# Scoring the last 64 keys in two row halves, and moving twelve PSUM copies from ScalarE to VectorE

## The chip, the cores and the metric

The kernel runs on 1 core of one Trainium2 chip. The metric is the time of one execution on the device, in microseconds (us), of which lower is better. The program ran three times; the profile is of a further execution of its own. Everything below is about one core with five engines: TensorE (PE, with its weight loads as PEld), VectorE (DVE), ScalarE (ACT), GpSimd (POOL) and SyncE (SP). All data is float32 at the interface; most products are made from "high" and "low" parts of type float32r (three products for one), the weights times v product in plain float32.

## What is computed

Sigmoid attention over 4 batches, 12 heads, 448 positions and head size 64, then two dense blocks on the 1792 x 768 result:

```
scores = q @ k.T / sqrt(64) - log(448)          # per batch and head
attn   = 1 / (1 + exp(-scores));  x = attn @ v  # x is 1792 x 768 after joining the heads
h = max(x @ w1, x @ w2, x @ w3);  y = h @ w_out             # first block, d_ff 768
h = y @ w_in;  sm = exp(h - max(h)) / (sum + 1e-9)          # second block, d_ff 1024
ln = normalise(h * sm) * g_ln;    out = ln @ w_out2
```

## The kernel before

The heads are taken in pairs: 24 pairs (6 per batch), each a **visit**, numbered 0 to 23 here. In SBUF a pair's q and k lie with head 0 in partitions 0 to 63 and head 1 in partitions 64 to 127 (64 dimensions each). The 448 keys are cut into blocks of 128: c = 0, 1, 2 are whole, and c = 3 holds the last 64 keys. The k array has 512 columns for this: columns 384 to 447 hold head 0's last keys with zeros in the lower half of the rows, columns 448 to 511 hold head 1's with zeros in the upper half.

For one visit the order on PE is: the four score blocks in the order 3, 0, 1, 2 (the function `scores`, lines 246 to 266), then the products with v (`attend`, line 278): blocks 1 and 2 of the pair before, then blocks 3 and 0 of this pair. A score block is three products (high-high, low-high, high-low). For c = 0, 1, 2 each is two matmuls (line 257), one per head on its own 64 rows of the array, into two PSUM banks; the two run side by side. For c = 3 each is one matmul over all 128 rows (line 253), since the zeros keep the heads apart, into one bank. The PSUM pool `ps_sc` has 3 buffers of two banks, so a visit's fourth score block needs the buffer of its first; `ps_av` has 2 buffers of one bank.

ACT turns each score block into weights `sf` with a sigmoid: 128 x 896 for c = 0, 1, 2 (line 265), 128 x 448 for c = 3 (line 262, with a buffer of its own). After a pair's last product with v, `take_x` (from line 286) takes the 128 x 448 result `av` out of PSUM: ACT writes its high part (B11h, B21h or B22h), DVE the low part (B11l, ...), and for the even batches (0 and 2) ACT also copies it to T1f or T4f in float32. For the odd batches DVE makes differences with those copies.

Between the two halves of the attention (visits 0 to 11 and 12 to 23) PE makes the product of two weight matrices, `pw` (line 469). Its operands `wi_t` and `r_wo` are prepared during visits 2 to 11: per piece one ACT instruction (line 155) and four on DVE (lines 159, 163, 54, 57), two pieces in a visit. Visit 12's scores stand inside the last part of `pw`. In the second half, background steps (splits of the T arrays, conversion of the last weights with pieces `w2s` that go out to DRAM through two staging buffers, conversion of the next group) are spread between the visits' steps.

PE, ACT and DVE run their instructions in the order in which the program is written. After the attention, from 201.20 us, come the Strassen-like products of the first block and the second block.

Of the kernel before, what the change touches and what calls it, by code (L numbers as in the profile page):

```python
# [7 lines left out]
F32 = mybir.dt.float32  # L8
F32R = mybir.dt.float32r
I32 = mybir.dt.int32  # L10
AF = mybir.ActivationFunctionType
# [5 lines left out]
P = 128  # L17
B, H, S, D = 4, 12, 448, 64
# [27 lines left out]
def sigmoid_attention_max_moe_solu_ln(tc, q, k, v, w123, wo, wi, w2, g, out):  # L46
    nc = tc.nc
    pe, act, dve, pool, sp = nc.tensor, nc.scalar, nc.vector, nc.gpsimd, nc.sync

    def copy(eng, dst, src):  # L50
        if eng is act:
            act.copy(dst, src)
        else:
            eng.tensor_copy(dst, src)

    def rest(eng, dst, src, hi):
        eng.tensor_tensor(out=dst, in0=src, in1=hi.bitcast(F32), op=ALU.subtract)  # L57

    def tt(dst, a, b, op):
        dve.tensor_tensor(out=dst, in0=a, in1=b, op=op)  # L60

    def open_pool(name, bufs, side="left", space=None):
        kw = dict(name=name, bufs=bufs, side=side)
        if space is not None:
            kw["space"] = space
        cm = tc.tile_pool(**kw)
        return cm, cm.__enter__()
# [22 lines left out]
    a_cm, apool = open_pool("apool", 2)  # L90
# [3 lines left out]
    bias_s = const.tile([P, 1], F32, name="bias_s")  # L94
# [111 lines left out]
    def f_tile(nm, i, name):  # L206
        return fpool.tile([P, S], F32, tag=f"{nm}_{i}", name=name)
# [16 lines left out]
    def load_v(pr):  # L224
        if pr >= NP:
            return
        vr = apool.tile([P, 2, 4, D], F32, tag="vr", name=f"vr{pr}", bufs=3)
        sp.dma_start(out=vr, in_=v[pr])
        v_ops[pr] = vr
# [16 lines left out]
    def scores(pr, c):  # L246
        qt, kt = qk_ops[pr]
        sc = ps_sc.tile([P, 2, 512], F32, tag="sc", name=f"sc{pr}_{c}")
        terms = ((0, 0), (1, 0), (0, 1))
        for t, (x, y) in enumerate(terms):  # L250
            start, stop = t == 0, t == len(terms) - 1
            if c == 3:
                pe.matmul(sc[:, 0, :S], lhsT=kt[:, x, c * P :], rhs=qt[:, y], start=start, stop=stop)
                continue
            for j in range(2):
                rows = slice(j * D, (j + 1) * D)
                pe.matmul(  # L257
                    sc[:, j, :S], lhsT=kt[rows, x, c * P : (c + 1) * P], rhs=qt[rows, y], start=start, stop=stop
                )
        if c == 3:  # L260
            sf = apool.tile([P, S], F32, tag="s3", name=f"sf{pr}_{c}", bufs=1)
            act.activation(sf, sc[:, 0, :S], AF.Sigmoid, bias=bias_s, scale=1.0 / math.sqrt(D))  # L262
        else:
            sf = apool.tile([P, 2, S], F32, tag="sf", name=f"sf{pr}_{c}", bufs=5)
            act.activation(sf, sc[:, :, :S], AF.Sigmoid, bias=bias_s, scale=1.0 / math.sqrt(D))  # L265
        weights[(pr, c)] = sf

    pas = {}
# [1 line left out]
    def attend(pr, n):  # L270
        vr = v_ops[pr]
        c = BLOCKS[n]
        if n == 0:
            pas[pr] = ps_av.tile([P, 512], F32, tag="av", name=f"av{pr}")
        pa = pas[pr]
        sf = weights.pop((pr, c))
        for j in range(2):
            pe.matmul(  # L278
                pa[j * D : (j + 1) * D, :S],
                lhsT=vr[:, j, c],  # L280
                rhs=sf if c == 3 else sf[:, j],
                start=(n == 0),
                stop=(n == 3),
            )
        if n == 3:
            v_ops.pop(pr)
            load_v(pr + 3)

    def take_x(pr):
        pa = pas.pop(pr)[:, :S]  # L290
        b, hp = divmod(pr, NPAIR)
        bp, odd = divmod(b, 2)
        half, i = divmod(hp, 3)
        f = {nm: fts.get((bp, nm, i)) for nm in TS}

        def new(nm):
            t = fts[(bp, nm, i)] = f_tile(nm, i, f"{nm}f{bp}_{i}")
            return t

        nm = (("B11", "B21"), (None, "B22"))[odd][half]  # L300
        if nm:
            hi, lo = xops[bp][(nm, i)]
            copy(act, hi, pa)
            rest(dve, lo, pa, hi)
        if not odd:
            copy(act, new("T4" if half else "T1"), pa)
        elif not half:
            copy(act, new("T3"), pa)
            tt(f["T1"], pa, f["T1"], ALU.subtract)
        else:  # L310
            t2 = new("T2")
            tt(t2, pa, f["T1"], ALU.subtract)
            tt(f["T3"], pa, f["T3"], ALU.subtract)
            tt(f["T4"], f["T4"], t2, ALU.subtract)
# [27 lines left out]
    def visit(pr, n_conv):  # L342
        for n, c in enumerate(BLOCKS):
            scores(pr, c)
            if n == 1:
                prep_qk(pr + 1)
        finish_conv()
        attend_rest(pr, n_conv)
# [12 lines left out]
    def attend_rest(pr, n_conv, steps=0):  # L361
        if pr > 0 and pr - 1 in pas:
            attend(pr - 1, 2)
            run_bg(steps)
            attend(pr - 1, 3)
            run_bg(steps)
            take_x(pr - 1)
        attend(pr, 0)
        run_bg(steps)
        attend(pr, 1)  # L370
        run_bg(steps)
        begin_conv(n_conv)
# [23 lines left out]
    attend(MID - 1, 3)  # L396
    finish_conv()
    take_x(MID - 1)
    assert not conv

# [84 lines left out]
    for fc in range(FC):  # L485
        for n in range(2):
            if (fc, n) == (FC - 1, 1):
                for i, c in enumerate(BLOCKS):
                    scores(MID, c)
                    if i == 1:  # L490
                        prep_qk(MID + 1)
            while not {("wo", fc, 0), ("wo", fc, 1)} <= ready:
                run_bg()
            gen_w(fc, n)
        slots.pop(("wo", fc, 0))
        slots.pop(("wo", fc, 1))
# [67 lines left out]
    for pr in range(MID + 1, NP):  # L564
        for n, c in enumerate(BLOCKS):
            scores(pr, c)
            if n == 1:
                prep_qk(pr + 1)
            run_bg()
        attend_rest(pr, 0, 1)  # L570
        run_bg(2)
    attend(NP - 1, 2)
    attend(NP - 1, 3)
    take_x(NP - 1)
    run_bg(1 << 20)
    for cm, _ in reversed(ps1):
# [449 lines left out]
```

## Time and profile before

| | before |
|---|---|
| median of 3 runs | 664.98 us (662.64 to 666.3) |
| the profiled execution | 661.11 us |
| span of its profile | 659.3 us |
| busy: PE, DVE, ACT | 650.7 us (99%), 484.0 us (73%), 318.4 us (48%) |

The span counts from the first recorded instruction to the last; the 1.8 us between 659.3 and 661.11 lie around it. Busy PE time says only that some matmul was in flight. The granted clock of TensorE was 1.00 in every slice.

### The profile page before, as it was taken

The numbers are of one execution on the slowest core, as the hardware profiler recorded it, in microseconds if no ns is written. First come the engines' busy times: TensorE is split into PE (matmuls) and PEld (weight loads), VectorE is DVE, ScalarE is ACT, GpSimd is POOL, SyncE is SP. The second block draws the span as 40 slices with busy tenths as digits, with TensorE's granted clock in tenths as the row PEclk, the third lists the DMA queues.
The fourth block names the chain that finished last, engine by engine and source line by source line (L and its number), as shares of the span: only waits on it lengthen the run. The fifth ranks groups of instructions, "written<-read, shape, count | busy, mean of one in ns | idle before, by whom it ended". The sixth has DMA issues, their size and how long they took to land.

```text
span 659.3 us, 9629 instructions
## 1 busy us (share of the span) xinstructions
PE 650.7 (99%) x3370; PEld 534.1 (81%) x3370; DVE 484.0 (73%) x1051; ACT 318.4 (48%) x642; POOL 58.0 (9%) x112
## 2 busy tenths in 40 slices
PE   9999999999999999999999999999999999999997
PEld 5555588754458999999999999978989898989897
DVE  4799988688758786775787577638959595868583
ACT  5888534587876534534444444315424242433242
POOL 1111121001110101100101100022000000000000
PEclk9999999999999999999999999999999999999999
DMA  8688769956540215534335422899743323323231
GB/s 295 215 261 255 214 208 330 325 179 197 162 128 1 96 67 175 167 113 134 106 108 205 120 70 91 286 357 408 273 143 99 115 93 116 99 77 115 61 113 48
DMA packets 53328, 109.16 MB, mean 166 GB/s; under 512 B 5952, under 2 KB 34656, under 8 KB 52512
## 3 DMA queue, kind: packets, MB, share of 16 engines
q1 hardware_dynamic: 44208, 64.48, 29.3%
q0 software_dynamic: 8928, 43.85, 20.3%
q8 instruction: 26, 0.43, 0.3%
q10 hardware_dynamic: 144, 0.23, 0.1%
q14 instruction: 22, 0.18, 0.1%
HBM read 76.29 MB, written 32.24 MB: 165 GB/s over the span
## 4 chain that ended last, share of the span: by engine, by line
PE 71%; DVE 15%; DMA 5%; ACT 4%; issue 4%; SPq 0%; ACTq 0%; DVEq 0%
PE x L604 17%; PE h L682 16%; PE v L604 9%; PE ox L874 8%; PE z L604 4%; PE av L278 4%; DMA wf<-w_d 3%; PE sc L257 3%; PE ov L874 2%; PE ow L874 2%; PE oz L874 2%; DVE y_wi L163 1%; ACT sf L265 1%; DVE qt L57 1%; DVE y_wo L163 1%
## 5 line engine op out<-in xcount | busy, mean ns | idle before, releaser
L682 PE MATMUL h<-wf,hh 128*128 128x512 f32 x336 | 104.0, 390 | 1.1 <-DMA wf<-w_d 0.9
L278 PE MATMUL av<-sf,vr 128*64 128x448 f32 x384 | 77.5, 545 | 0.0
L682 PEld LDWEIGHTS h<-wf,hh 128*128 128x128 f32 x336 | 62.7, 188 | 14.4 <-DMA wf<-w_d 1.9
L265 ACT ACTIVATE sf<-sc,bias_s 128x896 f32<-128x896 f32 x72 | 67.8, 1010 | 1.2
L682 PE MATMUL h<-wf,hl 128*128 128x512 f32 x168 | 65.4, 389 | 0.0
L278 PEld LDWEIGHTS av<-sf,vr 128*64 128x64 f32 x384 | 25.4, 136 | 40.9 <-issue 35.5
L257 PE MATMUL sc<-qt,kt 64*128 64x448 f32 x432 | 51.2, 376 | 2.1 <-ACT sf L262 2.0
L644 ACT COPY u<-x 128x448 f32<-128x448 f32 x36 | 19.2, 533 | 65.6 <-PE x L604 65.6
L147 POOL DMA_DIRECT2D raw<-in_w x52 | 28.3, 545 | 241.8 <-DVE S L57 126.4
L469 PE MATMUL pw<-wi_t,r_wo 128*128 128x512 f32 x216 | 49.6, 390 | 0.0
L257 PEld LDWEIGHTS sc<-qt,kt 64*128 64x128 f32 x432 | 38.7, 184 | 12.8 <-issue 5.9
L469 PEld LDWEIGHTS pw<-wi_t,r_wo 128*128 128x128 f32 x216 | 40.4, 188 | 9.4 <-issue 1.0
L772 DVE TENSOR_REDUCE st<-h 128x1 f32<-128x1024 f32 x14 | 17.0, 1216 | 36.3 <-PE h L682 36.3
L682 PEld LDWEIGHTS h<-wf,hl 128*128 128x128 f32 x168 | 31.5, 188 | 6.6 <-DVE hl L57 0.2
L604 PE MATMUL x<-B11h,A 128*128 128x448 f32 x108 | 33.7, 366 | 0.0
L604 PE MATMUL x<-T4h,A 128*128 128x448 f32 x108 | 33.7, 366 | 0.0
L604 PE MATMUL x<-T2h,S 128*128 128x448 f32 x108 | 33.6, 365 | 0.0
L604 PE MATMUL v<-T1h,S 128*128 128x448 f32 x108 | 33.6, 365 | 0.0
L604 PE MATMUL v<-B22h,S 128*128 128x448 f32 x108 | 33.6, 365 | 0.0
L604 PE MATMUL z<-B21h,A 128*128 128x448 f32 x108 | 33.6, 365 | 0.0
L604 PE MATMUL x<-T3h,S 128*128 128x448 f32 x108 | 33.6, 365 | 0.0
L874 PE MATMUL ox<-w2t,opS 128*128 128x384 f32 x168 | 32.2, 340 | 0.0
(160 smaller groups left out, 1386.4 us busy)
## 6 DMA issues: line engine op xcount, KB each, us to landing
raw<-in_w POOLq DMA_DIRECT2D x52, 384.0 KB, 3.8
w2t<-w_d POOLq DMA_DIRECT2D x12, 768.0 KB, 13.2
w_d<-w2s SPq DMA_DIRECT2D x42, 192.0 KB, 2.1
kr<-in_k SPq DMA_DIRECT2D x24, 256.0 KB, 3.5
vr<-in_v SPq DMA_DIRECT2D x24, 256.0 KB, 3.9
raw<-in_wi POOLq DMA_DIRECT2D x16, 384.0 KB, 4.5
w_d<-ws SPq DMA_DIRECT2D x12, 512.0 KB, 4.9
wf<-w_d SPq DMA_DIRECT2D x6, 1024.0 KB, 12.0
```

The source lines that it names most:

```text
L57: eng.tensor_tensor(out=dst, in0=src, in1=hi.bitcast(F32), op=ALU.subtract)
L147: pool.dma_start(out=t, in_=source(key).rearrange("p (n t) -> p n t", t=2))
L163: dve.scalar_tensor_tensor(out=yi, in0=raws[key][:, cols, 0], scalar=29, in1=yi, op0=ALU.logical_shift_right, op1=ALU.bitwise_or)
L257: pe.matmul(sc[:, j, :S], lhsT=kt[rows, x, c * P : (c + 1) * P], rhs=qt[rows, y], start=start, stop=stop)
L265: act.activation(sf, sc[:, :, :S], AF.Sigmoid, bias=bias_s, scale=1.0 / math.sqrt(D))
L278: pe.matmul(pa[j * D : (j + 1) * D, :S], lhsT=vr[:, j, c], rhs=sf if c == 3 else sf[:, j], start=(n == 0), stop=(n == 3),)
L469: pe.matmul(ps, lhsT=wt[:, a, cols], rhs=wi_t[:, b, c0 : c0 + 512], start=(i == 0), stop=(i == 3 * KC - 1))
L604: pe.matmul(ps, lhsT=l, rhs=r, start=(start and c == 0 and i == 0), stop=(stop and c == 2 and i == 2), skip_group_check=True)
L644: act.copy(e, ps)
L682: pe.matmul(h2s[t][:, n], lhsT=(hh, hl)[l][:, f], rhs=wfs[f // 3][:, f % 3, r, n * 512 : (n + 1) * 512], start=(f == 0 and i == 0), stop=( ...
L772: dve.tensor_reduce(out=nmax, in_=ps, axis=AX.XY, op=ALU.max, negate=True)
L874: pe.matmul(bank[b], lhsT=op[:, l, kc], rhs=wt[:, kc, :, c0 : c0 + OU], start=(start and kc == 0 and i == 0), stop=(stop and kc == 3 and i ...
```

## The change

`scores` no longer treats c = 3 apart: the last 64 keys are scored like the other blocks, by two matmuls per product on 64 rows each, with head 0's zero columns (or head 1's) beside its keys, and the sigmoid for them is 128 x 896. All four weight blocks of a pair now take buffers of the one tag `sf`, of which there are still 5; the separate buffer is gone. In `take_x` the float32 copy of the even batches, 12 in all, is made by DVE instead of ACT.

```diff
--- before.py
+++ after.py
@@ -249,20 +249,13 @@
         terms = ((0, 0), (1, 0), (0, 1))
         for t, (x, y) in enumerate(terms):
             start, stop = t == 0, t == len(terms) - 1
-            if c == 3:
-                pe.matmul(sc[:, 0, :S], lhsT=kt[:, x, c * P :], rhs=qt[:, y], start=start, stop=stop)
-                continue
             for j in range(2):
                 rows = slice(j * D, (j + 1) * D)
                 pe.matmul(
                     sc[:, j, :S], lhsT=kt[rows, x, c * P : (c + 1) * P], rhs=qt[rows, y], start=start, stop=stop
                 )
-        if c == 3:
-            sf = apool.tile([P, S], F32, tag="s3", name=f"sf{pr}_{c}", bufs=1)
-            act.activation(sf, sc[:, 0, :S], AF.Sigmoid, bias=bias_s, scale=1.0 / math.sqrt(D))
-        else:
-            sf = apool.tile([P, 2, S], F32, tag="sf", name=f"sf{pr}_{c}", bufs=5)
-            act.activation(sf, sc[:, :, :S], AF.Sigmoid, bias=bias_s, scale=1.0 / math.sqrt(D))
+        sf = apool.tile([P, 2, S], F32, tag="sf", name=f"sf{pr}_{c}", bufs=5)
+        act.activation(sf, sc[:, :, :S], AF.Sigmoid, bias=bias_s, scale=1.0 / math.sqrt(D))
         weights[(pr, c)] = sf
 
     pas = {}
@@ -278,7 +271,7 @@
             pe.matmul(
                 pa[j * D : (j + 1) * D, :S],
                 lhsT=vr[:, j, c],
-                rhs=sf if c == 3 else sf[:, j],
+                rhs=sf[:, j],
                 start=(n == 0),
                 stop=(n == 3),
             )
@@ -303,7 +296,7 @@
             copy(act, hi, pa)
             rest(dve, lo, pa, hi)
         if not odd:
-            copy(act, new("T4" if half else "T1"), pa)
+            copy(dve, new("T4" if half else "T1"), pa)
         elif not half:
             copy(act, new("T3"), pa)
             tt(f["T1"], pa, f["T1"], ALU.subtract)
```

On DVE at the end of visit 2 (`take_x` of pair 1; B11l is the low part, `av` the PSUM result, kt and qt the split k and q of pair 4, y_wi a piece of weight in work), before:

```order
L57 TENSOR_TENSOR B11l_1_122<-av_293,B11h_1_121 128x448
L54 CAST kt_375<-kr_261 128x512
L54 CAST qt_376<-qr_262 128x448
L57 TENSOR_TENSOR kt_375<-kr_261,kt_375 128x512
L57 TENSOR_TENSOR qt_376<-qr_262,qt_376 128x448
L159 TENSOR_SCALAR y_wi_0_356<-y_wi_0_356 128x384
```

and now:

```order
L57 TENSOR_TENSOR B11l_1_122<-av_299,B11h_1_121 128x448
L54 COPY T1f_1_358<-av_299 128x448
L54 CAST kt_387<-kr_267 128x512
L54 CAST qt_388<-qr_268 128x448
L57 TENSOR_TENSOR kt_387<-kr_267,kt_387 128x512
L57 TENSOR_TENSOR qt_388<-qr_268,qt_388 128x448
```

The copy stands between the low part and the operands of a later pair; six such copies stand in visits 1 to 6, and six in visits 13 to 18.

On ACT at the same place (sf_3 is the weights of c = 3), before:

```order
L52 CAST B11h_1_121<-av_293 128x448
L52 COPY T1f_1_349<-av_293 128x448
L155 ACTIVATE y_wi_0_356<-raw_224 128x384
L155 ACTIVATE y_wi_1_358<-raw_227 128x384
L262 ACTIVATE sf_3_364<-sc_3_360,bias_s 128x448
L265 ACTIVATE sf_0_373<-sc_0_366,bias_s 128x896
```

and now:

```order
L52 CAST B11h_1_121<-av_299 128x448
L155 ACTIVATE y_wi_0_365<-raw_227 128x384
L155 ACTIVATE y_wi_1_367<-raw_230 128x384
L258 ACTIVATE sf_3_376<-sc_3_369,bias_s 128x896
L258 ACTIVATE sf_0_385<-sc_0_378,bias_s 128x896
```

The copy is gone from ACT's order, and the sigmoid of c = 3 has twice the columns.

## Rows read from the trace of the kernel before

**Rows 1.** Busy time by stretch, all engines: three of the program's stretches.
```profile
4.67:77.14 72.47, 72.41 (x446) 38.10 (x445) 61.49 (x141) 57.42 (x83) 12.62 (x23) 1.00 0.80 256
129.72:201.20 71.48, 69.59 (x425) 35.66 (x424) 52.60 (x119) 54.73 (x87) 7.91 (x14) 1.00 0.51 161
201.20:659.30 458.10, 452.75 (x2252) 414.37 (x2250) 326.99 (x691) 180.25 (x416) 29.24 (x56) 1.00 0.41 139
```

**Rows 2.** Timeline of PE in visit 4: start, length, engine, line, operation, count.
```profile
27.66 0.47 PE L253 MATMUL sc<-qt,kt 128*128 128x448 f32 x1
...
28.47 0.47 PE L257 MATMUL sc<-qt,kt 64*128 64x448 f32 x2
...
28.78 0.56 PE L257 MATMUL sc<-qt,kt 64*128 64x448 f32 x4
...
30.20 0.36 PE L257 MATMUL sc<-qt,kt 64*128 64x448 f32 x2
...
30.49 0.59 PE L278 MATMUL av<-sf,vr 128*64 128x448 f32 x1
```

**Rows 3.** Visit 10 on PE and ACT (timeline), and the page's group of sigmoids.
```profile
64.47 2.09 PE L257 MATMUL sc<-qt,kt 64*128 64x448 f32 x18
...
64.64 0.64 ACT L262 ACTIVATE sf<-sc,bias_s 128x448 f32<-128x448 f32 x1 [0.90 <-PE sc L253]
65.39 2.80 ACT L265 ACTIVATE sf<-sc,bias_s 128x896 f32<-128x896 f32 x3
...
L265 ACT ACTIVATE sf<-sc,bias_s 128x896 f32<-128x896 f32 x72 | 67.8, 1010 | 1.2
```

**Rows 4.** Timelines of ACT and PE in visit 18, around its fourth score block.
```profile
164.42 0.36 ACT L52 CAST w2s<-raw 128x192 fp32r<-128x192 f32 x1 [1.89 <-DMA w_d<-w2s]
164.69 0.63 ACT L262 ACTIVATE sf<-sc,bias_s 128x448 f32<-128x448 f32 x1
...
165.37 0.68 PE L257 MATMUL sc<-qt,kt 64*128 64x448 f32 x4 [1.77 <-ACT sf L262]
...
165.68 0.58 PE L257 MATMUL sc<-qt,kt 64*128 64x448 f32 x4
```

**Rows 5.** Timeline of DVE, ends of visits 2 and 3.
```profile
20.84 0.62 DVE L57 TENSOR_TENSOR B11l<-av,B11h 128x448 fp32r<-128x448 f32 x1 [3.59 <-ACT B11h L52]
...
26.86 0.62 DVE L57 TENSOR_TENSOR B11l<-av,B11h 128x448 fp32r<-128x448 f32 x1
27.40 0.42 DVE L54 CAST kt<-kr 128x512 fp32r<-128x512 f32 x1
27.73 0.39 DVE L54 CAST qt<-qr 128x448 fp32r<-128x448 f32 x1
28.03 0.68 DVE L57 TENSOR_TENSOR kt<-kr,kt 128x512 fp32r<-128x512 f32 x1
```

**Rows 6.** Where the weight product begins: its first operand on DVE, its start on PE.
```profile
74.77 0.56 DVE L57 TENSOR_TENSOR r_wo<-y_wo,r_wo 128x384 fp32r<-128x384 f32 x1
...
77.14 8.50 PE L469 MATMUL pw<-wi_t,r_wo 128*128 128x512 f32 x36
```

**Rows 7.** Timeline of PE, fourth score block of visit 12.
```profile
124.61 0.87 PE L257 MATMUL sc<-qt,kt 64*128 64x448 f32 x6 [0.22 <-ACT sf L262]
```

**Rows 8.** Timeline of DVE between visits 14 and 17: three waits, and the w2s write.
```profile
138.86 0.36 DVE L60 TENSOR_TENSOR raw<-raw 128x192 f32<-128x192 f32 x1 [0.48 <-ACT raw L416]
...
149.03 0.62 DVE L57 TENSOR_TENSOR B11l<-av,B11h 128x448 fp32r<-128x448 f32 x1 [0.84 <-ACT B11h L52]
...
155.47 0.62 DVE L57 TENSOR_TENSOR B21l<-av,B21h 128x448 fp32r<-128x448 f32 x1 [0.79 <-ACT B21h L52]
...
160.20 0.35 DVE L57 TENSOR_TENSOR w2s<-raw,w2s 128x192 fp32r<-128x192 f32 x1
```

**Rows 9.** A copy that leaves ACT (visit 3), and visit 19's scores on PE.
```profile
27.51 0.53 ACT L52 COPY T1f<-av 128x448 f32<-128x448 f32 x1 [0.70 <-DVE B11l L57]
...
170.15 2.49 PE L257 MATMUL sc<-qt,kt 64*128 64x448 f32 x18
```

## The prediction, made before the changed kernel ran

> **What bounds the kernel now.** I first read the busy time by stretch [rows 1]. PE is busy in 72.41 of the first half's 72.47 us, in 69.59 of the second half's 71.48, and in 452.75 of the 458.10 us after the attention. So what moves PE's end of the attention moves the end of the program; the part after 201.20 us is untouched and only shifts. The reader should also see that in the two attention stretches DVE (61.49 and 52.60 us) and ACT (57.42 and 54.73) are not far behind PE, so a gain on PE can run into them. Then I read single instructions on the timelines.
>
> **PE, one visit.** The score part of visit 4 begins at 27.66 and ends where the products with v begin, 30.49 [rows 2]: 2.83 us. Of these the three full-row matmuls of c = 3 take 0.81 (27.66 to 28.47), the nine row-half pairs 2.02. The first step after a change of shape is long: 0.31 from 28.47 to 28.78, against (30.20 - 28.78) / 7 = 0.20 for the seven steps behind it; the last step, to the other shape, takes 0.29. With the change all four blocks are twelve equal pairs with one change of shape fewer: 0.31 + 10 x 0.20 + 0.29 = 2.60. That is **-0.23 us a visit**.
>
> Most of this does not stay, because the sigmoid of c = 3 doubles. The visit's fourth block needs the first block's PSUM buffer, so it waits for that sigmoid. From the first matmul of a block to the start of its sigmoid on a free ACT pass 0.92 us (64.47 to 65.39), and a 128 x 896 sigmoid takes 1.01 [rows 3]; PE resumed 0.05 us after such a sigmoid ended (164.69 + 0.63 = 165.32, then 165.37) [rows 4]. So the fourth block can start at 0.92 + 1.01 + 0.05 = 1.98 us into the visit, where PE would be ready at 0.31 + 8 x 0.20 = 1.91. The wait is 0.07, and a block that has waited begins with a long step again (165.37 to 165.68, 0.31 instead of 0.20) [rows 4], 0.11 more. Before, the 0.63 us sigmoid ended well ahead. So 0.18 of the 0.23 is given back: **-0.05 a visit**.
>
> **ACT.** Each visit gains 1.01 - 0.63 = 0.38 us of sigmoid. In the twelve visits with a copy, ACT loses its 0.53 and the 0.70 of wait for DVE in front of it [rows 9], so there ACT gets freer by some 0.8 us, and the sigmoid of c = 3 should not be late. In the other visits of the first half ACT had 0.90 us of idle time in front of that sigmoid [rows 3], which covers 0.38. I cost ACT at nothing there; without that cover it would be 0.38 a visit.
>
> **The price of a copy on DVE.** No row shows DVE copying from PSUM. The nearest from below is the cast of qt, same columns from SBUF: its successor starts 0.30 later (27.73 to 28.03). The nearest from above is the low part B11l, which reads the very same PSUM tile: 0.54 (26.86 to 27.40) [rows 5]. I take 0.54, since it is the same tile and columns, and keep 0.30. [...]
>
> **First half.** From 20.84 on DVE shows no wait until the weight product has begun [rows 5, 6]; it is a chain. Five copies are put on it (visits 2 to 6; visit 1's falls into the 3.59 us of wait before 20.84). The first r_wo piece is ready at 74.77 + 0.56 = 75.33 and PE starts on it at 77.14 [rows 6]: a slack of 1.81. With 5 x 0.54 = 2.70 it is ready at 78.03, and PE starts at 78.08, after waiting: **+0.94**, and PE's -0.05 per visit is lost in that wait. With 0.30 it is ready at 76.83 and the start is 76.88: -0.26. What is late on the way (the ACT steps on later pieces, which need DVE's work on earlier ones) costs PE less than this wait and is swallowed by it.
>
> **Second half.** Visit 12: its fourth block already waits for the sigmoid of c = 3, which ACT starts late [rows 7]; the sigmoid is 0.38 longer, so **+0.38**. Visit 18: ACT stands 1.89 us before a w2s cast for the staging buffer, whose data DVE wrote at 160.20 [rows 4, 8]; behind the cast stands the sigmoid of c = 3, and behind that PE's fourth block, which waited 1.77. So this block moves by 0.38 for the longer sigmoid and by what DVE's write at 160.20 moves. Four copies are in front of that write (take_x of pairs 12 to 15), 4 x 0.54 = 2.16. DVE's waits at 138.86 and 149.03, 0.48 + 0.84, were for ACT, which comes earlier by its copies, or absorb the delay; the 0.79 at 155.47 I let stand, since ACT's work in front of it hangs on DVE in its turn [rows 8]. That leaves 2.16 - 1.32 = 0.84, so **+1.22**, which takes in the few hundredths won in visits 13 to 17. With 0.30 a copy the delay is covered: +0.38. Visit 19: its half-row blocks took 2.49 against 2.09 (a late sigmoid) [rows 3, 9]; with ACT freer that goes: -0.40, and -0.05 as above, **-0.45**. Visits 20 to 23: 4 x -0.05 = **-0.20**.
>
> **Sum.** 0.94 + 0.38 + 1.22 - 0.45 - 0.20 = **+1.9 us** on the profiled execution's 661.11, so 663.0. The median of the runs is 3.9 above that execution, and the new median is to be set beside the old: 664.98 + 1.9 = **666.9 us**, 0.3% up. About 0.5%, 3.3 us here, is what a measurement of this kernel can tell from no change, so this is "no change", with the sign up. With copies of 0.30: -0.26 + 0.38 + 0.38 - 0.45 - 0.20 = -0.2, 664.8.
>
> **Rivals.** (1) *Slower: DVE becomes the bound of both halves.* DVE's waits in the second half were for ACT's high parts, and these now stand behind a sigmoid that is 0.38 longer; if ACT comes no earlier, the 1.32 us of waits stay and the w2s write moves by the full 2.16. If besides a copy takes the whole 0.62 of B11l instead of 0.54, nine copies on the two chains add 0.7. Sum 1.9 + 1.3 + 0.7 = +3.9, 668.9. It counts as slower when the two chains together move PE 1.4 us more than I have it. For it: the chain in the first half has no idle time at all. Against it: the copy's 0.53 and a 0.70 wait go from ACT in each of those visits [rows 9]. Chance 0.32.
>
> (2) *Faster: PE keeps what the shapes cost.* If ACT's sigmoid starts earlier than I read, or the fourth block's weights load during its wait, and DVE's copies find room, 22 visits give 22 x 0.23 = 5.1 us: 659.9. For it: the long steps at a change of shape are plain [rows 2]. Against it: the waiting block of visit 18 did begin with the long step [rows 4]. [...] Chance 0.08.
>
> (3) *The copy is cheap* (0.30): 664.8, as above, also "no change". Chance 0.18. That the row halves of c = 3 would not run side by side has next to no chance: shape and buffers are those of line 257.
>
> **How the numbers follow.** My forecast gets 0.42. No change: 0.42 + 0.18 = 0.60; slower 0.32; faster 0.08. The range takes in rivals 1 and 3 (668.9 and 664.8) and about 1 us of scatter of a median on either side, as the runs before scatter by 1.3 to 2.3: 663.8 to 670.2. It leaves out rival 2 and a worse case of rival 1.
>
> **What would show it.** Right: each visit's fourth score block shows a wait of about 0.1 us for the sigmoid of c = 3 and a 0.3 us step behind it; visits keep their 6.0 us; DVE's copy reads about 0.6 us with 0.54 to the next start; PE waits for r_wo at the start of pw, about 78; the waits at visits 12 and 18 grow to about 0.6 and 3. Wrong: no wait in front of fourth blocks (rival 2), copies of 0.39 us (rival 3), or pw beginning after 79 and visit 18's block more than 2 us later against its visit (rival 1).

## The result, and the profile after

The changed kernel takes 670.28 us (median of 6 runs, 668.98 to 672.27) beside 663.40 of the kernel before (6 runs, 660.92 to 666.3): a ratio of 1.0102, with a 95% interval of 1.0064 to 1.014. It is **slower by 1.0%**, some 7 us, where +1.9 us and "no change" were forecast; the median lies 0.08 us above the range. The profiled execution of the changed kernel took 671.73 us (span 669.9), 10.6 more than the one before (661.11); the last three experiments bear on why that is more than the medians' difference.

First the busy time by stretch of the changed kernel: the first half, visit 12's wait, what is behind it, visits 13 to 17, what is behind visit 18's wait, and the rest. The columns are those of [rows 1]: the stretch, its length, then busy time and count of PE, PEld, DVE, ACT and POOL, the granted clock, DMA share and GB/s.

```profile
4.67:77.82 73.15, 72.74 (x481) 37.88 (x481) 62.75 (x142) 58.74 (x79) 11.60 (x21) 1.00 0.77 246
...
122.96:127.91 4.95, 2.15 (x21) 1.54 (x20) 3.44 (x9) 3.76 (x9) 0.55 (x1) 0.96 1.01 353
127.91:137.62 9.71, 9.71 (x32) 6.32 (x32) 3.52 (x11) 3.93 (x7) 0.54 (x1) 0.67 0.71 237
137.62:168.53 30.91, 29.95 (x203) 15.86 (x202) 26.20 (x64) 25.07 (x38) 3.02 (x5) 1.00 0.47 150
...
174.57:180.17 5.60, 5.60 (x23) 2.00 (x23) 1.47 (x4) 4.80 (x8) 1.42 (x3) 0.70 0.34 110
...
211.90:669.90 458.00, 452.72 (x2252) 414.41 (x2250) 326.88 (x692) 180.22 (x416) 29.24 (x56) 1.00 0.41 139
```

The last row is 458.00 us, as before (458.10 in [rows 1]): all of the loss lies in the attention, which ends at 211.90 instead of 201.20. The first half lost only 0.68 (77.82 against 77.14). The two short rows with a granted clock of 0.67 and 0.70 are what the forecast had no term for: behind two waits the granted clock fell, and in the 9.71 and 5.60 us of those rows matmuls are long. The 18 of the weight product behind the first wait last 628 ns in the median, where those from 77.82 on, at a clock of 1.00, last 389; the 16 products with v behind the second last 819 ns, in visit 18 before the change 539.

The timeline of PE in the changed kernel at those places (start, length, engine, line, operation, count, and the idle time before it with what ended it):

```profile
77.82 4.41 PE L462 MATMUL pw<-wi_t,r_wo 128*128 128x512 f32 x18 [0.19 <-DVE r_wo L54]
...
122.96 2.14 PE L254 MATMUL sc<-qt,kt 64*128 64x448 f32 x18
127.91 1.49 PE L254 MATMUL sc<-qt,kt 64*128 64x448 f32 x6 [2.81 <-ACT sf L258]
129.32 6.72 PE L462 MATMUL pw<-wi_t,r_wo 128*128 128x512 f32 x18
...
137.62 2.86 PE L254 MATMUL sc<-qt,kt 64*128 64x448 f32 x24
...
158.06 0.89 PE L254 MATMUL sc<-qt,kt 64*128 64x448 f32 x6 [0.52 <-ACT sf L258]
...
164.57 0.87 PE L254 MATMUL sc<-qt,kt 64*128 64x448 f32 x6 [0.45 <-ACT sf L258]
...
168.53 2.09 PE L254 MATMUL sc<-qt,kt 64*128 64x448 f32 x18
174.57 0.89 PE L254 MATMUL sc<-qt,kt 64*128 64x448 f32 x6 [3.95 <-ACT sf L258]
175.39 4.85 PE L271 MATMUL av<-sf,vr 128*64 128x448 f32 x16
180.17 2.87 PE L254 MATMUL sc<-qt,kt 64*128 64x448 f32 x24
```

The fourth score block of visit 12 waited 0.22 us in [rows 7]; it now waits 2.81, and its own six matmuls take 1.49 instead of 0.87. Visit 18's waits 3.95 instead of 1.77 [rows 4]. Put in order, the shift of each mark against the profile before:

| mark on PE | before | after | later by | added here |
|---|---|---|---|---|
| visit 12, scores begin | 122.19 | 122.96 | 0.77 | 0.77 |
| visit 12, fourth block | 124.61 | 127.91 | 3.30 | 2.53 wait |
| visit 13 begins | 131.37 | 137.62 | 6.25 | 2.95 lower clock |
| visit 18 begins | 161.31 | 168.53 | 7.22 | 0.97: 1.10 in visits 16 and 17, which now wait, less 0.13 won in visits 13 to 15 |
| visit 18, fourth block | 165.37 | 174.57 | 9.20 | 1.98 wait |
| visit 19 begins | 169.34 | 180.17 | 10.83 | 1.63 lower clock |
| visit 20 begins | 175.72 | 186.12 | 10.40 | -0.43 |
| attention ends | 201.20 | 211.90 | 10.70 | 0.30 |

Why does ACT's sigmoid come so late in visit 12? The timeline of DVE in the changed kernel, at the first copy, where the chain begins, at the first operand of the weight product (the cast of L54 makes its high part, L57 its low part), in visit 12, and in the second half:

```profile
15.68 0.61 DVE L54 COPY T1f<-av 128x448 f32<-128x448 f32 x1
16.21 0.41 DVE L54 CAST kt<-kr 128x512 fp32r<-128x512 f32 x1
...
21.14 0.62 DVE L57 TENSOR_TENSOR B11l<-av,B11h 128x448 fp32r<-128x448 f32 x1 [3.08 <-ACT B11h L52]
...
77.31 0.36 DVE L54 CAST r_wo<-y_wo 128x384 fp32r<-128x384 f32 x1
77.71 0.56 DVE L57 TENSOR_TENSOR r_wo<-y_wo,r_wo 128x384 fp32r<-128x384 f32 x1
...
126.97 0.69 DVE L57 TENSOR_TENSOR ws<-pw,ws 128x512 fp32r<-128x512 f32 x1
...
156.70 0.62 DVE L57 TENSOR_TENSOR B11l<-av,B11h 128x448 fp32r<-128x448 f32 x1 [1.75 <-ACT B11h L52]
...
168.89 0.35 DVE L57 TENSOR_TENSOR w2s<-raw,w2s 128x192 fp32r<-128x192 f32 x1
```

The chain starts 0.30 later (21.14 against 20.84 in [rows 5]) and gets five copies, of which each moves what is behind it by 0.53 (15.68 to 16.21); `r_wo` is at 77.71 instead of 74.77 [rows 6], 2.94 later. And that lateness is still there 50 us on: DVE's low part of `ws`, at 124.05 before, is at 126.97, 2.92 later. In between, DVE and ACT feed each other, and nothing gives the time back: from 77 us to there DVE waits nine times in both kernels, each time for ACT and each time for 0.65 to 0.89 us, while ACT for its part waits for DVE, 29.1 us in all over that stretch (22.8 before). The timeline of ACT in visit 12, before:

```profile
123.44 0.58 ACT L52 CAST ws<-pw 128x512 fp32r<-128x512 f32 x1
123.92 0.64 ACT L262 ACTIVATE sf<-sc,bias_s 128x448 f32<-128x448 f32 x1
```

and after, there and in visits 15 and 18:

```profile
126.36 0.58 ACT L52 CAST ws<-pw 128x512 fp32r<-128x512 f32 x1
126.84 2.81 ACT L258 ACTIVATE sf<-sc,bias_s 128x896 f32<-128x896 f32 x3
...
153.89 0.37 ACT L52 CAST w2s<-raw 128x192 fp32r<-128x192 f32 x1 [1.55 <-DMA w_d<-w2s]
...
173.25 0.36 ACT L52 CAST w2s<-raw 128x192 fp32r<-128x192 f32 x1 [4.62 <-DVE qt L57]
173.51 1.00 ACT L258 ACTIVATE sf<-sc,bias_s 128x896 f32<-128x896 f32 x1
```

The sigmoid on which visit 12's fourth block waits stands on ACT behind the `ws` cast, and that stands behind steps that need DVE. So it came 2.92 us later (126.84 against 123.92) and was 0.37 longer: 3.29, while PE itself was only 0.77 late.

In visit 18 ACT stands before a `w2s` cast, as it did before the change [rows 4]. The profile puts the end of this wait to DVE (`qt`); but the chain of work that ends last between 166 and 176 us comes to the cast from the transfer of a `w2s` piece, which runs from 169.64 to 173.17; before the change, between 158 and 167 us, it comes from one that runs from 160.95 to 164.34. And the cast starts 4.36 us after DVE's `w2s` write (168.89 to 173.25), before the change 4.22 (160.20 to 164.42). So it's read here, too, as the wait for a staging buffer.

### The profile page after: what moved, and what is told of

Read it like the earlier page. It is cut to its first block, busy times and chain, and to the rows that moved or that the text cites. A ratio compares the mean times of both kernels' runs of the same rounds, so it can differ in the third digit from the quotient of the medians.

```text
span 669.9 us, 9820 instructions
## 1 busy us (share of the span) xinstructions
PE 655.2 (98%) x3442; PEld 536.4 (80%) x3442; DVE 490.0 (73%) x1063; ACT 320.8 (48%) x630; POOL 58.0 (9%) x112
## 4 chain that ended last, share of the span: by engine, by line
PE 68%; DVE 18%; DMA 5%; issue 4%; ACT 4%; SPq 0%; ACTq 0%; DVEq 0%
PE x L597 17%; PE h L675 16%; PE v L597 8%; PE ox L867 8%; PE z L597 4%; DMA wf<-w_d 3%; PE av L271 3%; PE sc L254 3%; PE ov L867 2%; PE ow L867 2%; PE oz L867 2%; DVE y_wi L163 1%; DVE qt L57 1%; ACT sf L258 1%; DMA w_d<-w2s 1%
## 5 line engine op out<-in xcount | busy, mean ns | idle before, releaser
L258 ACT ACTIVATE sf<-sc,bias_s 128x896 f32<-128x896 f32 x96 | 91.4, 1007 | 18.8 <-PE sc L254 16.0
L254 PE MATMUL sc<-qt,kt 64*128 64x448 f32 x576 | 71.2, 382 | 8.2 <-ACT sf L258 7.9
L254 PEld LDWEIGHTS sc<-qt,kt 64*128 64x128 f32 x576 | 50.6, 186 | 35.6 <-ACT sf L258 16.0
L271 PE MATMUL av<-sf,vr 128*64 128x448 f32 x384 | 79.1, 555 | 0.0
L462 PE MATMUL pw<-wi_t,r_wo 128*128 128x512 f32 x216 | 51.9, 403 | 0.2 <-DVE r_wo L54 0.2
L462 PEld LDWEIGHTS pw<-wi_t,r_wo 128*128 128x128 f32 x216 | 42.0, 196 | 10.5 <-PE av L271 0.9
```

The source lines that it names most:

```text
L254: pe.matmul(sc[:, j, :S], lhsT=kt[rows, x, c * P : (c + 1) * P], rhs=qt[rows, y], start=start, stop=stop)
L271: pe.matmul(pa[j * D : (j + 1) * D, :S], lhsT=vr[:, j, c], rhs=sf[:, j], start=(n == 0), stop=(n == 3),)
L462: pe.matmul(ps, lhsT=wt[:, a, cols], rhs=wi_t[:, b, c0 : c0 + 512], start=(i == 0), stop=(i == 3 * KC - 1))
```

## The experiments

The first four kernels ran together on one chip, 11 to 12 runs each; the kernel before had a median of 666.15 us there (34 runs, 660.67 to 668.92). The theory called A holds that the copies on DVE's chain make the wait at visit 12 and the fall of the clock behind it; B, that the longer sigmoid does.

**Row halves without the copies.** Scores and sigmoid as in the change; the copies stay on ACT.

```diff
-            copy(dve, new("T4" if half else "T1"), pa)
+            copy(act, new("T4" if half else "T1"), pa)
```

> The change's row halves and 128 x 896 sigmoid for c = 3, but the twelve copies stay on ACT. Theory A (the copies on DVE are the cost: five of them shift DVE's chain by 2.7 us, which arrives at visit 12 as a wait long enough for TensorE's clock to fall): pw starts at 77 +- 0.5, PE's wait at visit 12 is about 0.6 us (0.22 + 0.38), the clock stays at 1.00 around it; but ACT, already full in the visits with a copy, makes these visits about 6.35 instead of 6.0 us, so +3 to +4 us over before. Theory B (the longer sigmoid of c = 3 is the cost): visit 12 waits 2.5 us or more, the clock falls there, and the kernel is +6 us or more over before.

666.03 us, ratio 1.0014 (0.999 to 1.0038): no change. PE's timeline:

```profile
31.00 0.87 PE L254 MATMUL sc<-qt,kt 64*128 64x448 f32 x6 [0.34 <-ACT sf L258]
...
79.64 2.56 PE L462 MATMUL pw<-wi_t,r_wo 128*128 128x512 f32 x10
...
127.33 0.87 PE L254 MATMUL sc<-qt,kt 64*128 64x448 f32 x6 [0.48 <-ACT sf L258]
...
168.65 0.87 PE L254 MATMUL sc<-qt,kt 64*128 64x448 f32 x6 [1.75 <-ACT sf L258]
```

With the copies still on ACT the longer sigmoid does reach PE: waits of 0.34 in the early visits, and `pw` begins at 79.64, 2.5 later, where 77 had been expected. But the wait at visit 12 is 0.48, that of visit 18 is 1.75 (before the change 1.77), and behind them the granted clock stays at 1.00 (122 to 130 and 165.3 to 171.3 us). B is out as the cause of the two long waits. It isn't free of cost, though: in this profile the attention ends at 205.15, 3.95 us later than in the profile before, which is the +3 to +4 that was expected, and which the medians don't show.

**The copies alone.** c = 3 as before; the copies on DVE.

```diff
-            copy(act, new("T4" if half else "T1"), pa)
+            copy(dve, new("T4" if half else "T1"), pa)
```

> Scores of c = 3 as before, only the twelve copies by DVE. Theory A: DVE's r_wo is 2.7 us later and pw starts at about 77.9; visit 12's fourth block waits 2.4 to 2.8 us and the clock falls behind it; +5 to +8 us over before in all. Theory B: visits stay at 6.0 us, no wait over 1 us at visit 12, within 1 us of before.

669.26 us, ratio 1.0068 (1.0037 to 1.0098). PE's timeline, then two stretches behind the waits by busy time and clock:

```profile
78.26 3.97 PE L469 MATMUL pw<-wi_t,r_wo 128*128 128x512 f32 x16 [0.38 <-DVE r_wo L54]
...
127.98 0.87 PE L257 MATMUL sc<-qt,kt 64*128 64x448 f32 x6 [2.42 <-ACT sf L262]
...
169.93 0.89 PE L257 MATMUL sc<-qt,kt 64*128 64x448 f32 x6 [2.99 <-ACT sf L262]
```

```profile
127.98:134.80 6.82, 6.82 (x33) 4.32 (x33) 3.95 (x12) 3.91 (x7) 0.54 (x1) 1.00 0.91 290
169.93:175.61 5.68, 5.68 (x22) 1.98 (x23) 2.08 (x6) 4.70 (x8) 1.62 (x3) 0.70 0.37 136
```

The copies alone make both waits, 2.42 and 2.99. In this profile the clock fell behind the second only: so a wait of this size does not always cost it. A holds for the waits; the clock had to be tried by itself.

The attention ends at 207.08 here, 5.88 us later than in the profile before, against 10.70 with the whole change. So in these profiles, one of each kernel, the row halves add 4.8 us to what the copies cost: 0.39 to the wait at visit 12, the fall of the clock behind it (2.95), and the waits in visits 16 and 17, which this kernel doesn't have. The copies make the two long waits, but they aren't the whole loss.

**One batch's copies back on ACT**, the other parts as in the change: batch 0's (visits 1 to 6), then batch 2's (visits 13 to 18).

```diff
-            copy(dve, new("T4" if half else "T1"), pa)
+            copy(dve if bp else act, new("T4" if half else "T1"), pa)
```

> The change, but the six copies of the first half (batch 0) are made by ACT again. Theory A: visit 12's wait is about 0.6 us without a fall of the clock (some 5.5 us less there than with the change), visits 2 to 6 take about 6.35 us (+1.8), the second half is as with the change (a wait of some 4 us at visit 18 and a clock fall behind it): +4 to +6 us over before, 1 to 3 us faster than the change. Theory B: same as the change within 1 us.

```diff
-            copy(dve, new("T4" if half else "T1"), pa)
+            copy(act if bp else dve, new("T4" if half else "T1"), pa)
```

> The change, but the six copies of the second half (batch 2) are made by ACT again. Theory A: the first half and visit 12 as with the change (wait 2.8 us, clock falls, visit 13 starts at about 137.6); in the second half no copies on DVE, so DVE's w2s write moves less, but ACT is full, visits 14 to 18 take 6.35 us, and visit 18 waits 2 to 3 us: +6 to +9 us over before. Theory B (the longer sigmoid): same as the change or slower, +7 to +10; told from A only by where visit 18's wait ends.

667.99 us, ratio 1.0029 (1.0005 to 1.0053), and 669.71, ratio 1.0062 (1.004 to 1.0084). The fourth blocks of visits 12 and 18, first with batch 0's copies on ACT:

```profile
127.20 0.87 PE L254 MATMUL sc<-qt,kt 64*128 64x448 f32 x6 [0.46 <-ACT sf L258]
...
170.04 0.87 PE L254 MATMUL sc<-qt,kt 64*128 64x448 f32 x6 [4.22 <-ACT sf L258]
```

and with batch 2's there:

```profile
128.07 0.87 PE L254 MATMUL sc<-qt,kt 64*128 64x448 f32 x6 [2.79 <-ACT sf L258]
...
172.42 0.89 PE L254 MATMUL sc<-qt,kt 64*128 64x448 f32 x6 [2.00 <-ACT sf L258]
```

Each batch's copies make the wait of their own half: 0.46 against 2.79 at visit 12, 2.00 against 4.22 at visit 18. The times are not sums of parts, since copies on ACT bring back the 0.34 waits and the late `pw` (79.51 in the first of the two).

**Filling the waits.** To tell the wait from the clock, PE got work to do while it waits, with results that are overwritten: 12 matmuls ahead of visit 12's fourth block, then 18 more in visit 18. (The edits shown leave out the lines that hand the PSUM buffer on to its later user.) The next four kernels ran together on another chip, 5 to 12 runs each; the kernel before had 664.42 there (17 runs, 660.23 to 666.87). Theory C holds the clock's fall for a cost of its own: the work behind the waits is long because the clock is down, to 0.67 and 0.70 above. D holds something else for the cause. The changed kernel ran again beside them.

> The changed kernel once more, unaltered, so that the fills can be set beside it on the same chip. Both theories: a median near 670.3, 7 us above the kernel before; fourth score block of visit 12 waits 2.8 us, that of visit 18 about 4.0 us, and behind each the granted clock of the next stretch is 0.67 to 0.70.

671.00 us, ratio 1.0112 (1.0086 to 1.0137); waits of 2.80 and 3.84, as before.

```diff
...
+                    if i == 3:
+                        ps = pws[(fc, n)] = ps_av.tile([P, 512], F32, tag="av", name=f"pw{n}_{fc}")
+                        for _ in range(12):
+                            qt, kt = qk_ops[MID]
+                            pe.matmul(ps[:, :S], lhsT=kt[:, 0, :P], rhs=qt[:, 0], start=True, stop=True)
                     scores(MID, c)
```

> The changed kernel with 12 matmuls of 128 rows and 448 columns on PE ahead of visit 12's fourth score block; their result goes to a bank that the weight product overwrites. They take 12 x 0.27 = 3.2 us at the most (0.81 us for three such matmuls before the change) and fill the wait of 2.81 us. [...] Theory D (what is long behind the wait is long for another reason: operands, PSUM, the order of the work): visit 13 begins at 137.6 or, with 0.4 us of added work, at 138.0, and the time stays at 670.3 or rises.

669.03 us, 2.0 under the changed kernel. PE's timeline, and the stretch from the fourth block to visit 13:

```profile
125.04 2.70 PE L488 MATMUL pw<-qt,kt 128*128 128x448 f32 x12
127.91 0.87 PE L254 MATMUL sc<-qt,kt 64*128 64x448 f32 x6 [0.17 <-ACT sf L258]
128.71 4.38 PE L464 MATMUL pw<-wi_t,r_wo 128*128 128x512 f32 x18
...
171.25 1.49 PE L254 MATMUL sc<-qt,kt 64*128 64x448 f32 x6 [4.51 <-ACT sf L258]
```

```profile
127.91:134.68 6.77, 6.77 (x33) 4.28 (x34) 3.53 (x11) 3.91 (x7) 0.54 (x1) 1.00 0.95 310
```

The block starts at the same instant, 127.91, since ACT sets it. But the stretch behind it takes 6.77 us at a clock of 1.00 instead of 9.71 at 0.67: 2.94 us come back for doing useless work. Some of it is lost again at visit 18, which is reached earlier and waits 4.51, with the clock falling behind it (0.62 from 171.25 to 177.43; its six matmuls take 1.49). C holds: 2.0 us of the 2.94 show in the time, which D had stay or rise.

```diff
+            if pr == 18 and n == 3:
+                early_pa = ps_av.tile([P, 512], F32, tag="av", name=f"av{pr}")
+                for _ in range(18):
+                    qt, kt = qk_ops[pr]
+                    pe.matmul(early_pa[:, :S], lhsT=kt[:, 0, :P], rhs=qt[:, 0], start=True, stop=True)
...
```

> As the fill at visit 12, and 18 further matmuls of 128 rows and 448 columns ahead of visit 18's fourth score block, into the bank that this visit's products with v then overwrite: 18 x 0.2 to 0.27 = 3.6 to 4.9 us, in a wait of 3.95. Theory C: the products with v behind the block take 3.2 instead of 4.85 us, and visit 19 begins 1.6 us earlier after visit 18's start than in the changed kernel, less what the 18 matmuls take over the 3.95 (0 to 0.9): a further 0.7 to 1.6 us, to about 666.4; attention ends near 207.5 instead of 211.9. Theory D: no gain over the fill at visit 12 alone, or a loss of up to 0.9.

666.72 us, 4.3 under the changed kernel, ratio to the kernel before 1.0057 (1.0035 to 1.0079). Visit 18 to 19, timeline and stretch:

```profile
167.00 3.94 PE L570 MATMUL av<-qt,kt 128*128 128x448 f32 x18
171.36 0.87 PE L254 MATMUL sc<-qt,kt 64*128 64x448 f32 x6 [0.41 <-ACT sf L258]
172.16 3.23 PE L271 MATMUL av<-sf,vr 128*64 128x448 f32 x16
```

```profile
171.36:175.32 3.96, 3.96 (x24) 1.54 (x24) 0.80 (x3) 3.96 (x7) 0.39 (x2) 1.00 0.23 80
```

From block to visit 19 it is 3.96 instead of 5.60 us, and the attention ends at 207.1 (expected 207.5). The clock is worth 4.3 us of the loss by the medians, and 4.6 by the table above. The mean granted clock of each run agrees: 0.992 to 0.995 in the changed kernel beside it, 0.999 or 1.000 in all six with both waits filled, 0.997 to 1.000 in the kernel before.

**A third staging buffer in the kernel before.** Visit 18's wait there is for a `w2s` buffer [rows 4]; a buffer of the weights makes room.

```diff
-            sf = apool.tile([P, 2, S], F32, tag="sf", name=f"sf{pr}_{c}", bufs=5)
+            sf = apool.tile([P, 2, S], F32, tag="sf", name=f"sf{pr}_{c}", bufs=4)
...
-            return stp.tile([P, 2 * QU], F32, tag="stg", name=name, bufs=2)
+            return stp.tile([P, 2 * QU], F32, tag="stg", name=name, bufs=3)
```

> The kernel before with three staging buffers for the w2s pieces instead of two, and four buffers for the weights instead of five to make room. Theory C (the wait at visit 18 is for a staging buffer, as the 1.89 us on ACT ahead of the w2s cast says): visit 18's wait of 1.77 falls to under 0.5 us and the time by 1.3 to 2, to about 0.3% under the kernel before. Rival: four weight buffers are too few, PE's score blocks or ACT's sigmoids wait for the products with v of the pair before, and the time rises by 1 us or more; or the next transfer is waited for instead, and nothing changes.

663.38 us (659.53 to 664.47), ratio 0.9985 (0.9966 to 1.0004): nothing that can be told from no change. The wait at visit 18 is gone (the 0.2 us that PE still waits for the sigmoid of c = 3 are those of visit 12), and its attention ends at 199.82 instead of 201.20. Yet its span is 662.2, and behind the attention it takes 4.2 us longer than the 458.10 of [rows 1]. A group of the first block's products shows why; the columns are duration min/median/max in ns and first and last start. The kernel before:

```profile
L604 PE MATMUL x<-B11h,A x108: 362/365/471, 201.2 to 416.3; 128*128 128x448 f32 x108
```

and with three staging buffers:

```profile
L604 PE MATMUL x<-B11h,A x108: 368/368/475, 199.8 to 419.2; 128*128 128x448 f32 x108
```

The same 108 matmuls are spread over 219.4 us instead of 215.1, at a granted clock of 1.00 in both.

**The kernel before, three further profiles.** Is that what scatters its runs by 8 us?

> The kernel before, unaltered, for a further profile. Its runs scatter from 660.2 to 668.9 us, those of the changed kernel by 2 to 3 us. Theory F (the scatter lies in the products of the first block: their 1134 matmuls take 231.2 us from first to last start in the profile before, and 235.6 in the one of the third staging buffer): if this run is near 661 to 662, they take 231.2; if it is near 665 to 667, they take 235.6, and the attention ends at 201.2 as before. Theory G (the scatter is in the attention, in waits or in the granted clock): a run near 666 shows an attention that ends 4 us later, and 231.2 for these products.

> As the first further profile of the kernel before: theory F wants 231.2 us for the first block's 1134 matmuls in a run near 661 and 235.6 in one near 666, with the attention's end at 201.2 in both; theory G wants a later end of the attention in the longer run.

> As the first further profile of the kernel before: theory F wants 231.2 us for the first block's 1134 matmuls in a run near 661 and 235.6 in one near 666, with the attention's end at 201.2 in both; theory G wants a later end of the attention in the longer run.

They took 667.04, 666.05 and 663.76 us; the 1134 matmuls take 235.63, 235.64 and 231.19 from first to last start, the attention ends at 202.6, 201.3 and 203.1. The first of the three:

```profile
L604 PE MATMUL x<-B11h,A x108: 368/368/475, 202.6 to 422.0; 128*128 128x448 f32 x108
```

```profile
165.70 1.49 PE L257 MATMUL sc<-qt,kt 64*128 64x448 f32 x6 [1.92 <-ACT sf L262]
```

```profile
165.70:171.19 5.49, 5.49 (x22) 2.16 (x23) 1.71 (x5) 3.95 (x7) 1.61 (x3) 0.70 0.31 87
```

F holds for 4.4 us of the scatter: two of the four profiles of the kernel before have the longer first block. The rest is of G's kind: in the first and third of the three the clock falls behind visit 18's wait, of 1.92 and 1.97 us (0.70 in the row above, and 0.72 from 165.3 to 171.3 in the third), and the attention ends later. The profile before, with 1.77, and the second, with 1.70, kept the clock at 1.00. So the profile on which the forecast was worked out was one of the shortest executions, and the lower clock behind visit 18 isn't the change's alone: the kernel before pays it in some executions, 1.5 us in the first of the three (5.49 against 3.97).

All eight profiles that contain the change or a part of it are short behind the attention: 457.2 to 459.8 us to the end of the span, as in the two of the kernel before with the shorter first block (458.1 and 458.9), where the two with the longer one take 462.7 and 462.9. So these eight, too, have the shorter first block. If that holds in their other runs, the medians understate what the attention lost, and the record fits that: each of these kernels lies 2.8 to 5.0 us nearer to the kernel before by its median than by the end of the attention in its profile (row halves alone -0.1 against 3.95, copies alone 3.1 against 5.88, the change 6.9 against 10.70). That is argued from one profile of each, not shown. Why the first block runs in two ways isn't known.

## Why the prediction was right or wrong

**The number came near, the working did not.** The sign was right, and 670.28 lies only 0.08 us above the range. That is no credit to the sum. The range reaches so high because the slower rival and 1 us of scatter were taken in, and the medians' 6.9 us are smaller than what the change did to the attention in the profiles, 10.70, where the sum had 1.9.

**The step that failed: visit 12, "so +0.38".** The text took the chain's delay as settled at the start of `pw`: 2.70 late, 1.81 of it slack, the rest a wait. But a slack that one meeting point has is not time that the chain gets back. DVE and ACT stayed 2.92 late until visit 12, where [rows 7] already showed a wait, which means no slack at all. The sum there should have been 2.92 + 0.37 less the 0.77 by which PE was late itself: 2.5, as measured. The sentence "what is late on the way costs PE less than this wait and is swallowed by it" holds at `pw`, where PE would have been 0.49 late by itself (77.82 - 0.19 - 77.14); the mistake is that the account ends there.

**The term that was missing: the clock.** Waits were costed at their own length. Behind 2.81 and 3.95 us of waiting PE then lost 2.95 and 1.63 more, at granted clocks of 0.67 and 0.70; filling the waits gave 4.3 us of the time back. Nothing in the prediction weighed the clock, though the forecast itself gave visit 18 a wait of 3 us.

**Visit 18, +1.22: measured 1.98.** The `w2s` cast came 1.61 later against its visit (173.25 - 164.42 - 7.22), and the sigmoid behind it was 0.37 longer. DVE's `w2s` write moved by 8.69 (160.20 to 168.89), that is by 2.44 against visit 13, and by 1.47 against visit 18, for which 0.84 had been put. The four copies are 2.1 of the 2.44. The waits for ACT did not shrink as forecast: of the three in [rows 8] the one of 0.48 went and the one of 0.79 stayed, but the one of 0.84 became 1.75. In front of it ACT stood 1.55 us for a staging buffer in visit 15 (153.89), where it had no such wait before; the sigmoid of visit 16, which stands behind it, then kept PE waiting 0.52. This is the mechanism of the rival "DVE becomes the bound of both halves". Visits 16 and 17 now wait for 0.97 in all, where a few hundredths of gain had been put. The -0.20 of visits 20 to 23 came out at +0.30: visit 21 waits 0.23, and the others gain nothing.

**PE's -0.05 a visit** came in part. Visit 13 to 14 is 5.95 us (137.62 to 143.57); in the first half most visits stay at 6.00, because the sigmoid of c = 3 starts 0.98 us into a visit (27.75 to 28.73), not 0.92, and visits 9 and 10 take 6.10, with that sigmoid at 1.09 (57.75 to 58.84). It cost nothing against the forecast there, since `pw` waits for DVE.

**Right:** the copy's price, 0.61 us long with the next start 0.53 later (forecast 0.54), so the rival with 0.30 fell; visit 19, -0.43 for -0.45. The faster rival fell because the score part of a visit takes 2.78 us at best (143.57 to 146.35), not the 2.60 of shapes without a wait.

**Near by luck: the start of `pw`,** 77.82 for a forecast 78.08, after a wait for `r_wo`. The prediction took the low part in [rows 6] for the operand that PE waits for. After the change that part ends at 77.71 + 0.56 = 78.27, when `pw` has begun. PE waits for the cast ahead of it, which ended 0.15 us before `pw` (77.31 + 0.36 = 77.67). Before, it stood here on DVE:

```profile
74.37 0.36 DVE L54 CAST r_wo<-y_wo 128x384 fp32r<-128x384 f32 x1
```

With the same 0.15 the slack was 77.14 - 74.88 = 2.26, not 1.81, and the lateness was 2.94, not 2.70, since the chain began 0.30 later. The two errors partly cancel: 0.68 came for 0.94.

By its terms: 0.94, 0.38, 1.22, -0.45, -0.20 were forecast; 0.77, 2.53, 1.98, -0.43, 0.30 came, and 0.97 and 4.58 for which there was no term. The slower rival had the sign and one of the places; its sum of +3.9 lacked visit 12 and the clock.

## What to carry to other kernels

When work is added to a chain of two engines that feed each other, follow its lateness to every later place where a third engine meets it, and ask at each how much slack is there; slack at the first meeting says nothing of the second. Then ask of each new wait on TensorE what the clock does behind it: here the clock cost 2.95 us behind a wait of 2.81, and work with no use was cheaper than idling there.

## What the runs showed of the hardware

- TensorE's granted clock fell behind waits of 2.81 and 3.95 us (the changed kernel; 0.67 and 0.70 in the stretch behind), 2.80 and 3.84 (its second profile; 0.68 and 0.70), 2.99 (the copies alone; 0.70), 4.22 (batch 0's copies on ACT; 0.72 from 170 to 176 us), 2.79 and 2.00 (batch 2's there; the 18 matmuls of `pw` behind the first took 5.97 us, where they take 4.38 at 1.00, and the clock from 170 to 176 was 0.78), 4.51 (visit 12's wait filled; 0.62), 1.92 and 1.97 (the kernel before; 0.70 and 0.72). Behind 1.70 and 1.77 (the kernel before), 1.75 (the row halves alone) and 2.42 (the copies alone) it stayed at 1.00. At visit 12 the fall came behind 2.79 to 2.81 and not behind 2.42, at visit 18 behind 1.92 to 4.51 and not behind 1.70 to 1.77. So the length of the wait alone doesn't decide it; what else does, no run here shows. With the idle time filled down to 0.17 and 0.41 us it stayed at 1.00.
- The fall need not begin at once: behind 2.81 us the six score matmuls already took 1.49 us (clock 0.50); behind 3.95 they took 0.89 as usual (0.94), and only the products with v were long (4.85 instead of 3.23).
- One and the same program, the kernel before, ran its 1134 matmuls of 448 columns in 231.2 us (the profile before) or in 235.6 (the second further one) at a mean granted clock of 1.000 in both (365 or 368 ns in the median rows, 204 or 208 from start to start). The difference is 0.7% of the whole time, more than the 0.3% that was forecast for this change. Why it happens is open.
